# Linear attention with a dense layer, twice over: query tiles earlier in the last blocks, the last one behind the sums

## The chip, the core and the metric

The kernel runs on one core of one Trainium2 chip. The metric is the device time of one execution in microseconds (us). PE is TensorE, DVE is VectorE, ACT is ScalarE, POOL is GpSimd, SP is SyncE, which only issues DMAs here.

## The reference

Two layers follow one another twice (A, B, A, B), each with a residual. A is linear attention with the hedgehog feature map, B is dense, mish, dense. S = 2048 rows, D = 640, H = 32 heads of 20, F = 1536, everything in float32.

```python
def A(x, wqkv, w_phi, wo):
    q, k, v = split_heads(x @ wqkv)                   # 32 heads of 20
    pq, pk = q @ w_phi, k @ w_phi                     # per head, 20 x 20
    phi_q = concat(softmax(pq), softmax(-pq))         # 40 features a head
    phi_k = concat(softmax(pk), softmax(-pk))
    kv, z = phi_k.T @ v, phi_k.sum(rows)              # sums over all 2048 rows
    return merge_heads((phi_q @ kv) / (phi_q @ z + 1e-6)) @ wo

def B(x, w1, b1, w2):
    return mish(x @ w1 + b1) @ w2                     # mish: x * tanh(softplus(x))
...
# each layer's output is added to its input; a layer norm without weights stands before each
```

## The kernel before

Every product of float32 numbers is made of three matmuls of halves: a value is split into a high and a low part, and h times wh, h times wl and l times wh are summed in PSUM (`project_half`, L408 to L415). A projection of one tile of 128 rows has 2 halves of columns, 5 slices of the inner dimension and 3 products: 30 matmuls.

The 2048 rows are 8 blocks (NB) of 2 tiles (BT), tile number i from 0 to 15. Attention runs in two passes, since the averages need the sums over all keys. The first pass, `attend_first`, goes over the blocks. Each block has six pieces of work: key tiles k0 and k1, value tiles v0 and v1, query tiles q0 and q1. The tuple `order` says in which order PE projects them. The product with `w_phi` has been folded into the key and query weights at the start (`fold_part`, `fold_high`, `fold_low`, the section under `written()`).

Each piece is a generator. Its first step projects. `features` then takes five steps: ACT copies the projection out of PSUM into the tile `e`; DVE takes maximum and minimum, and POOL (queries) or DVE (keys) subtracts; ACT takes the exponential; DVE sums and inverts; POOL multiplies. `advance()` moves every pending generator by one step for each new piece. A key tile ends with 32 small matmuls into `kva` (L488), a PSUM bank that holds the sums over all keys. A query tile ends with a transpose on DVE and four stores by SP to the DRAM buffer `e_d` (L505).

What sets the order around the change:

- In `attend_first` a scheduler puts the instructions of each engine in order; `issue_after` ties one behind another. In the section under `written()` and, for PE and SP, in the second pass, the order is that of the code.
- PSUM has two double-bank tiles for projections (`mm_tile`) and four single banks (`one_tile`), one of which is `kva` during the first pass.
- Query tiles use two SBUF buffers, one for even and one for odd tiles (`query_tile`), so tile i reuses that of tile i - 2.
- In the last block `order` leaves out q1. The generator `rest()` (L687) projects this last query tile in pieces, which the second pass calls up between its own steps with `next(rest)`.

The second pass, `attend_second` (L740), begins with `finish_kv`: ACT copies `kva`, PE transposes it in three pieces (L731), DVE multiplies them by a mask into `kvb` (L734). `average(b, t)` then has 44 small matmuls (L764) with the query features that were loaded back from `e_d` (`load_groups`, L716), and DVE divides. After it come the projection with `wo`, the residual and the norm for layer B.

Of the kernel before, what the change touches and what calls it, by code (L numbers as in the profile page):

```python
# [21 lines left out]
DH = 20  # L22
# [3 lines left out]
BT = 2  # L26
# [18 lines left out]
def kernel(  # L45
# [412 lines left out]
    def attend_first(layer, x_src, first):  # L458
# [16 lines left out]
                except StopIteration:  # L475
                    pending.remove(g)

        def keys(xts, i, v):
            e = big_tile()
            yield from features(project(xts, i % BT, kv_ws, 0, w=QC), e, False)  # L480
            yield
            if i % BT == 0 and BT < i < NT - BT:
                yield
            for r in range(9):
                for j in range(4):
                    h = 3 * (4 * (r // 3) + j) + r % 3
                    if h < H:
                        nc.tensor.matmul(kva[32 * j:32 * j + DH + 1, 40 * r:40 * r + 40],  # L488
                                         v[:, (DH + 1) * h:(DH + 1) * (h + 1)], e[:, 40 * h:40 * h + 40],
                                         start=(i == 0 and r == 0), stop=(i == NT - 1), skip_group_check=True)  # L490

        def queries(xts, i, ps=None):
            e = query_tile(i)
            yield from features(project(xts, i % BT, q_ws, 0, w=QC) if ps is None else ps, e, True)

            b, t = divmod(i, BT)
            if i == NT - BT - 1:
                yield
                with tc.issue_after(last_recip[0]):
                    nc.vector.transpose(e, e)  # L500
            else:
                nc.vector.transpose(e, e)
            dst = e_d[b].rearrange("(j f) (t q s) -> t q f j s", f=32, t=BT, s=32)
            for q in range(4):
                nc.sync.dma_start(dst[t, q], e[32 * q:32 * q + 32].rearrange("f (j s) -> f j s", s=32))  # L505
                if b == NB - 1:
                    yield
# [15 lines left out]
        if first is None:  # L523
            with written():
                xt = fetch(x_src, 0)
                bd = big_tile()[:120, :720].rearrange("p (t c) -> p t c", t=6)
                nc.sync.dma_start(bd[:, :3], phi_bd[:, :3])
                raw_q = load_raw(0, range(3))

                nc.vector.memset(bd[:80, 5, :80], 0.0)  # L530
                nc.sync.dma_start(bd[:40, 5, :40], phi_bd[80:120, 4, 80:120])
                nc.sync.dma_start(bd[40:80, 5, 40:80], phi_bd[:40, 5, :40])
                nc.sync.dma_start(bd[:, 3:5], phi_bd[:, 3:5])
                shift_phi(bd, slice(0, 3))
                raw_q += load_raw(0, range(3, 6))
                kv_ws = [r1_pair(k) for k in range(KD)]
                raw_v = [fetch_v(k) for k in range(KD)]
                raw = load_raw(1)
                early = fetch(x_src, 1)
                mvs = [norm_stats(t, xt) for t in range(BT)]  # L540
                norm_scale(0, mvs)
                shift_phi(bd, slice(3, 5))
                shift_phi(bd, 5)

                q_ws = [r2_pair(k) for k in range(KD)]
                mm = [mm_tile(), mm_tile()]
                pcs = [mm[0][:, 0], mm[0][:, 1], mm[1][:, 0], mm[1][:, 1], one_tile()]
                for t in range(3):
                    for k in range(KD):
                        fold_part(pcs[k], k, t, bd, raw_q)  # L550
                xn = [row_tile() for _ in range(BT)]
                act(xn[0], xt[:, 0, :], AF.Identity, bias=stats[:, 0, 1, 0:1], scale=stats[:, 0, 0, 0:1])
                nc.vector.tensor_scalar(xn[1], xt[:, 1, :], stats[:, 0, 0, 1:2], stats[:, 0, 1, 1:2],
                                        op0=ALU.mult, op1=ALU.add)

                def highs(c, ks):
                    for k in ks:
                        fold_high(q_ws, pcs[k], k, c)

                def lows(c, ks):  # L560
                    for k in ks:
                        fold_low(q_ws, pcs[k], k, c)

                def make_v(k, low):
                    split(kv_ws[k][0][:, D:2 * D], kv_ws[k][1][:, D:2 * D], raw_v[k], low)

                def half(c, ks):
                    project_half(q0[c], nxt, 0, q_ws, 0, c, ks, w=QC)

                highs(0, (0, 1))  # L570
                lows(0, (0, 1))
                nxt = Transposed(xn)
                nxt.turn(one_tile())
                nxt.high()
                nxt.lower()
                highs(0, (4,))
                lows(0, (4,))
                pcs[0], pcs[1] = one_tile(), one_tile()
                for k in (0, 1):
                    fold_part(pcs[k], k, 3, bd, raw_q)  # L580
                mm = mm_tile()
                nxt.turn(mm[:, 0])
                nxt.turn(mm[:, 1])
                highs(0, (2,))
                nxt.high()
                highs(0, (3,))
                nxt.high()
                lows(0, (2, 3))
                nxt.lower()
                nxt.lower()  # L590
                for t in (4, 5):
                    for k in (0, 1):
                        fold_part(pcs[k], k, t, bd, raw_q)
                highs(1, (0, 1))
                q0 = [one_tile()]
                half(0, (0, 1))
                mm = mm_tile()
                pcs[2], pcs[3] = mm[:, 0], mm[:, 1]
                for k in (2, 3):
                    for t in range(3, 6):  # L600
                        fold_part(pcs[k], k, t, bd, raw_q)
                lows(1, (0, 1))
                half(0, (2, 3))
                make_v(0, nc.gpsimd)
                highs(1, (2, 3))
                lows(1, (2, 3))
                pcs[4] = one_tile()
                for t in range(3, 6):
                    fold_part(pcs[4], 4, t, bd, raw_q)
                half(0, (4,))  # L610
                make_v(1, nc.gpsimd)
                highs(1, (4,))
                lows(1, (4,))
                q0.append(one_tile())
                half(1, range(KD))
                for k in (2, 3, 4):
                    make_v(k, nc.vector)
            nc.sync.dma_start(mask, bass.AP(tensor=head_mask.tensor, offset=head_mask.offset,
                                            ap=[[1, 120], [120 * (DH + 1), 3]]))
        else:  # L620
            nxt, kv_ws, turn = first
            with tc.issue_after(last_load[0]):
                load_k_weights(kv_ws)
            q_ws = load_q_weights()
        for b in range(NB):
            xts = nxt
            order = ("k0", "k1", "v0", "v1", "q0", "q1")
            if b == 0 and layer:
                order = ("v0", "k0", "k1", "v1", "q0", "q1")
            elif b == 0:  # L630
                order = ("q0", "v0", "v1", "k0", "q1", "k1")
            elif b == 1 and not layer:
                order = ("k0", "q0", "k1", "v0", "q1", "v1")
            elif b == NB - 1:
                order = ("k0", "k1", "v0", "v1", "q0")
            vs = [v_tile() for _ in range(BT)]
            if 2 <= b < 2 + KD and not layer:
                with tc.issue_after(last_act[0]):
                    o_ws.append(next(o_gen))
                spill_o_weights(b - 2, o_ws[-1])  # L640
            for n, (kind, t) in enumerate(order):
                t = int(t)
                i = b * BT + t
                if b == 0 and layer == 0 and n in (2, 3):
                    fold_phi(kv_ws, bd, raw, ((0, 0), (1, 0), (2, 0), (3, 0)) if n == 2 else
# [8 lines left out]
                if b + 1 < NB:  # L654
# [3 lines left out]
                        nxt = xt if layer else normed(b + 1, xt)  # L658
                    elif n > 2:
                        nxt.step()  # L660
                g = {"k": lambda: keys(xts, i, vs[t]), "q": lambda: queries(xts, i, q0 if i == 0 and not layer else None),
                     "v": lambda: values(xts, i, vs[t])}[kind]()
                if b == 0 and not layer:
                    with tc.issue_after(last_product[0]):
# [21 lines left out]

        def rest():  # L687

            ps = [one_tile(), one_tile()]
            project_half(ps[0], xts, 1, q_ws, 0, 0, w=QC)  # L690
            advance()
            advance()
            yield
            project_half(ps[1], xts, 1, q_ws, 0, 1, range(2), w=QC)
            yield
            project_half(ps[1], xts, 1, q_ws, 0, 1, range(2, 4), w=QC)
            yield
            project_half(ps[1], xts, 1, q_ws, 0, 1, range(4, KD), w=QC)
            pending.append(queries(xts, NT - 1, ps))
            next(pending[-1])  # L700
            while pending:
# [38 lines left out]
    def attend_second(x_src, x_dst, acc, fetches, makes, fetch_next, begin_next):  # L740
# [61 lines left out]
        with tc.manual_schedule(engines={mybir.EngineType.PE, mybir.EngineType.SP}):  # L802
# [1 line left out]
            next(rest)  # L804
            next(kv)
            loaded[1] = begun[0] + load_groups(1, 5) + begun[1]
            next(rest)
            next(kv)
            next(rest)
            average(0, 0)  # L810
# [303 lines left out]
```

## Time and profile before

| | |
|---|---|
| runs | 1360.11, 1357.13, 1360.85 us, median 1360.11 |
| the profiled execution's own time | 1360.29 us |
| its span | 1358.5 us |
| mean granted clock of PE | 0.999 |
| instructions in the span | 30980 |
| DMA | 174.11 MB, mean 128 GB/s |

The span is what the profiler saw of the execution, from the first instruction to the last; 1.8 us lie around it. Busy times are sums over an engine's instructions, and a line number is a line of the kernel. In the view of waits a row says which engine stood still at which line, what it waited for, how long in all, how often, and the longest. The word "issue" stands where the trace shows nothing that it waited for. In the view of time a row begins with start and length, and in brackets stand the idle time before it and what ended it. SPq is the queue of SP, and its rows are the issues of DMAs. In the view of stretches the columns are the stretch, its length, busy time and number of instructions of PE, PEld (loading of weights), DVE, ACT and POOL, the granted clock, the DMA share and GB/s. The first pass of layer 0 ends near 247 us, that of layer 1 near 907 us.

### The profile page before, as it was taken

The numbers are of one execution on the slowest core, as the hardware profiler recorded it, in microseconds if no ns is written. First come the engines' busy times: TensorE is split into PE (matmuls) and PEld (weight loads), VectorE is DVE, ScalarE is ACT, GpSimd is POOL, SyncE is SP. The second block draws the span as 40 slices with busy tenths as digits, with TensorE's granted clock in tenths as the row PEclk, the third lists the DMA queues.
The fourth block names the chain that finished last, engine by engine and source line by source line (L and its number), as shares of the span: only waits on it lengthen the run. The fifth ranks groups of instructions, "written<-read, shape, count | busy, mean of one in ns | idle before, by whom it ended". The sixth has DMA issues, their size and how long they took to land.

```text
span 1358.5 us, 30980 instructions
## 1 busy us (share of the span) xinstructions
PE 1349.6 (99%) x12896; PEld 1339.3 (99%) x12896; DVE 1058.6 (78%) x1797; ACT 576.1 (42%) x968; POOL 466.2 (34%) x419
## 2 busy tenths in 40 slices
PE   9999999999999999999999999999999999999999
PEld 9999999999999999999999999989999999999998
DVE  5988988886787888778768888778668776677775
ACT  5444444322554555455443344332236444454443
POOL 3355544434322222122226556634251211111112
PEclk9999999999999999999999999999999999999999
DMA  9544444797613443334574435456974221333200
GB/s 335 162 101 91 94 113 98 183 298 271 217 28 88 117 117 88 55 93 113 147 224 97 114 79 102 86 141 215 285 254 132 78 65 41 90 98 97 68 31 20
DMA packets 352629, 174.11 MB, mean 128 GB/s; under 512 B 287449, under 2 KB 324041, under 8 KB 352489
## 3 DMA queue, kind: packets, MB, share of 16 engines
q1 hardware_dynamic: 352489, 172.14, 46.7%
q8 instruction: 101, 1.65, 0.5%
q14 instruction: 39, 0.32, 0.1%
HBM read 106.23 MB, written 65.86 MB: 127 GB/s over the span
## 4 chain that ended last, share of the span: by engine, by line
PE 93%; DVE 5%; POOL 1%; DMA 1%; issue 0%; ACT 0%; SPq 0%; POOLq 0%; DVEq 0%
PE mm L414 25%; PE one L889 25%; PE mm L940 24%; PE one L414 11%; PE mm L764 2%; PE one L334 2%; PE one L488 2%; DVE r L448 1%; PE one L940 1%; DMA raw<-in_w 1%; DVE xn L777 1%; DVE m L439 0%; PE mm L263 0%; PE one L92 0%; DVE r L442 0%
## 5 line engine op out<-in xcount | busy, mean ns | idle before, releaser
L940 PE MATMUL mm<-r2h,ol 128*128 128x320 f32 x1240 | 296.1, 309 | 0.0
L915 POOL TENSOR_TENSOR ol<-big,ol 128x512 fp32r<-128x512 f32 (+1 forms) x98 | 130.9, 1336 | 477.9 <-ACT ol L914 419.7
L889 PE MATMUL one<-xtl,r1h 128*128 128x256 f32 x960 | 268.2, 279 | 0.0
L889 PE MATMUL one<-xth,r1l 128*128 128x256 f32 x960 | 268.0, 279 | 0.0
L889 PE MATMUL one<-xth,r1h 128*128 128x256 f32 x960 | 265.9, 279 | 0.0
L940 PEld LDWEIGHTS mm<-r2h,ol 128*128 128x128 f32 x1240 | 212.5, 188 | 0.0
L940 PE MATMUL mm<-r2l,ol 128*128 128x320 f32 x620 | 191.2, 309 | 0.0
L414 PE MATMUL mm<-r1h,xth 128*128 128x304 f32 (+1 forms) x600 | 185.1, 309 | 0.0
L414 PE MATMUL mm<-r1l,xth 128*128 128x304 f32 (+1 forms) x600 | 183.8, 306 | 0.0
L414 PE MATMUL mm<-r1h,xtl 128*128 128x304 f32 (+1 forms) x600 | 183.5, 306 | 0.2 <-POOL xtl L351 0.2
L889 PEld LDWEIGHTS one<-xtl,r1h 128*128 128x128 f32 x960 | 180.4, 188 | 0.0
L889 PEld LDWEIGHTS one<-xth,r1l 128*128 128x128 f32 x960 | 180.4, 188 | 0.0
L889 PEld LDWEIGHTS one<-xth,r1h 128*128 128x128 f32 x960 | 179.6, 188 | 0.0
L904 DVE TENSOR_SCALAR big<-big 128x512 f32<-128x512 f32 (+1 forms) x98 | 57.2, 583 | 110.0 <-ACT big L902 109.8
L906 ACT ACTIVATE big<-big,two 128x512 f32<-128x512 f32 (+1 forms) x98 | 70.1, 716 | 116.1 <-DVE big L905 116.1
L914 ACT ACTIVATE ol<-big 128x512 fp32r<-128x512 f32 (+1 forms) x98 | 60.9, 622 | 137.6 <-DVE big L913 137.5
L902 ACT ACTIVATE big<-one,b1s 128x256 f32<-128x256 f32 x192 | 80.8, 467 | 89.4 <-PE one L889 88.9
L450 POOL TENSOR_TENSOR r<-r,r 128x1280 f32<-128x1280 f32 x32 | 77.2, 2411 | 116.6 <-DVE r L449 88.5
L940 PEld LDWEIGHTS mm<-r2l,ol 128*128 128x128 f32 x620 | 116.5, 188 | 0.0
L414 PEld LDWEIGHTS mm<-r1h,xth 128*128 128x128 f32 x600 | 112.8, 188 | 0.9
L414 PEld LDWEIGHTS mm<-r1h,xtl 128*128 128x128 f32 x600 | 112.8, 188 | 0.4 <-POOL xtl L351 0.4
L414 PEld LDWEIGHTS mm<-r1l,xth 128*128 128x128 f32 x600 | 112.8, 188 | 0.1
(160 smaller groups left out, 3148.9 us busy)
## 6 DMA issues: line engine op xcount, KB each, us to landing
e_d<-r SPq DMA_DIRECT2D x128, 160.0 KB, 4.1
big<-e_d SPq DMA_DIRECT2D x32, 640.0 KB, 7.2
x_d<-xt SPq DMA_DIRECT2D x23, 640.0 KB, 4.5
xt<-x_d SPq DMA_DIRECT2D x22, 640.0 KB, 4.9
n_d<-xn SPq DMA_DIRECT2D x168, 80.0 KB, 2.4
xt<-in_x SPq DMA_DIRECT2D x16, 640.0 KB, 4.3
xn<-x_d SPq DMA_DIRECT2D x28, 320.0 KB, 4.3
v<-n_d SPq DMA_DIRECT2D x30, 256.0 KB, 3.0
```

What stands on the lines that cost most here:

```text
L334: nc.tensor.transpose(ps[:, c, t * P:(t + 1) * P], self.rows[t][:, (c0 + c) * P:(c0 + c + 1) * P], ident)
L414: last_product[0] = nc.tensor.matmul(ps[:, :w], a[:, sl], r, start=(k == 0 and n == 0), stop=(k == KD - 1 and n == 2)).ins
L450: nc.gpsimd.tensor_tensor(eg, eg, r.unsqueeze(2).to_broadcast([P, 2 * H, DH]), op=ALU.mult)
L488: nc.tensor.matmul(kva[32 * j:32 * j + DH + 1, 40 * r:40 * r + 40], v[:, (DH + 1) * h:(DH + 1) * (h + 1)], e[:, 40 * h:40 * h + 40], start ...
L764: nc.tensor.matmul(po[c][64 * q:64 * q + 64, GW * j:GW * j + w], phs[g][:n, s0:s0 + 64], kvb[:n, g, :w], start=True, stop=True)
L889: nc.tensor.matmul(ph[:, j, :], l, r, start=(n == 0), stop=(n == 3 * KD - 1))
L902: exps[0] = nc.scalar.activation(part(ta, 0)[:, j - js.start], ph[:, j, :], AF.Exp, bias=b1s[:, 2 * pr + j:2 * pr + j + 1]).ins
L904: nc.vector.tensor_scalar_min(e, e, E_CAP)
L906: nc.scalar.activation(r, n, AF.Ln, bias=two)
L914: nc.scalar.activation(ah[:, js], n, AF.Copy)
L915: nc.gpsimd.tensor_tensor(al[:, js], n, ah[:, js].bitcast(F32), op=ALU.subtract)
L940: ins = nc.tensor.matmul(pys[t][c][:, :HC], (ah, ah, al)[n][:, j, t * P:(t + 1) * P], w, start=(f == 0 and n == 0), stop=(f == KF - 1 and ...
```

## The change

Three parts. First, the last four blocks get their own orders, with query tiles further ahead. Keys of the first tile of block 6 take two more idle steps before their sums, so that the value tile they need is there (`keys` now takes the list `vs` and reads it at that time). The value tiles of the last block are allocated later. The separate late transpose of tile 13 goes.

Second, `rest()` no longer projects a half tile ahead of the last key sums. The 30 matmuls now stand behind them, in pieces of 9, 9 and 12, and one call of `next(rest)` falls away.

Third, in the start section the first chunk of the query fold takes a single bank and the others the two double tiles; before, the last chunk had the single bank. The splits and transposes are put in another order to fit.

```diff
-        def keys(xts, i, v):
+        def keys(xts, i, vs):
             e = big_tile()
             yield from features(project(xts, i % BT, kv_ws, 0, w=QC), e, False)
             yield
             if i % BT == 0 and BT < i < NT - BT:
-                yield
+                for _ in range(3 if i == NT - 2 * BT else 1):
+                    yield
...
-                                         v[:, (DH + 1) * h:(DH + 1) * (h + 1)], e[:, 40 * h:40 * h + 40],
+                                         vs[i % BT][:, (DH + 1) * h:(DH + 1) * (h + 1)], e[:, 40 * h:40 * h + 40],
...
             b, t = divmod(i, BT)
-            if i == NT - BT - 1:
-                yield
-                with tc.issue_after(last_recip[0]):
-                    nc.vector.transpose(e, e)
-            else:
-                nc.vector.transpose(e, e)
+            nc.vector.transpose(e, e)
...
-                pcs = [mm[0][:, 0], mm[0][:, 1], mm[1][:, 0], mm[1][:, 1], one_tile()]
+                pcs = [one_tile(), mm[0][:, 0], mm[0][:, 1], mm[1][:, 0], mm[1][:, 1]]
...
-                highs(0, (0, 1))
-                lows(0, (0, 1))
+                highs(0, (0, 1, 2))
+                lows(0, (0,))
                 nxt = Transposed(xn)
                 nxt.turn(one_tile())
                 nxt.high()
+                lows(0, (1, 2))
                 nxt.lower()
-                highs(0, (4,))
-                lows(0, (4,))
+                highs(0, (3, 4))
                 pcs[0], pcs[1] = one_tile(), one_tile()
                 for k in (0, 1):
                     fold_part(pcs[k], k, 3, bd, raw_q)
-                mm = mm_tile()
-                nxt.turn(mm[:, 0])
-                nxt.turn(mm[:, 1])
-                highs(0, (2,))
-                nxt.high()
-                highs(0, (3,))
-                nxt.high()
-                lows(0, (2, 3))
-                nxt.lower()
-                nxt.lower()
+                nxt.turn(one_tile())
                 for t in (4, 5):
                     for k in (0, 1):
                         fold_part(pcs[k], k, t, bd, raw_q)
+                last = mm_tile()
+                nxt.turn(last[:, 0])
+                nxt.high()
+                nxt.high()
+                lows(0, (3, 4))
+                nxt.lower()
+                nxt.lower()
...
-                pcs[4] = one_tile()
+                pcs[4] = last[:, 1]
...
-            elif b == NB - 1:
-                order = ("k0", "k1", "v0", "v1", "q0")
-            vs = [v_tile() for _ in range(BT)]
+            elif b >= NB - 4:
+                order = (("k0", "k1", "v0", "q0", "q1", "v1"), ("k0", "k1", "q0", "q1", "v0", "v1"),
+                         ("k0", "q0", "q1", "k1", "v0", "v1"), ("k0", "k1", "q0", "v0", "v1"))[b - NB]
+            vs = []
...
+                if n == (3 if b == NB - 1 else 0):
+                    vs += [v_tile() for _ in range(BT)]
...
         def rest():
 
-            ps = [one_tile(), one_tile()]
-            project_half(ps[0], xts, 1, q_ws, 0, 0, w=QC)
             advance()
             advance()
+            ps = [one_tile(), one_tile()]
+            project_half(ps[0], xts, 1, q_ws, 0, 0, range(3), w=QC)
             yield
-            project_half(ps[1], xts, 1, q_ws, 0, 1, range(2), w=QC)
+            project_half(ps[0], xts, 1, q_ws, 0, 0, range(3, KD), w=QC)
+            project_half(ps[1], xts, 1, q_ws, 0, 1, range(1), w=QC)
             yield
-            project_half(ps[1], xts, 1, q_ws, 0, 1, range(2, 4), w=QC)
-            yield
-            project_half(ps[1], xts, 1, q_ws, 0, 1, range(4, KD), w=QC)
+            project_half(ps[1], xts, 1, q_ws, 0, 1, range(1, KD), w=QC)
             pending.append(queries(xts, NT - 1, ps))
...
             loaded[1] = begun[0] + load_groups(1, 5) + begun[1]
-            next(rest)
             next(kv)
```

More of the change, by code (lines that the diff above doesn't have):

```diff
@@ L660, in attend_first @@
                         nxt.step()
-                g = {"k": lambda: keys(xts, i, vs[t]), "q": lambda: queries(xts, i, q0 if i == 0 and not layer else None),
+                g = {"k": lambda: keys(xts, i, vs), "q": lambda: queries(xts, i, q0 if i == 0 and not layer else None),
                      "v": lambda: values(xts, i, vs[t])}[kind]()
```

## The prediction

> **What bounds the kernel now.** The page's engine line comes first, then the waits of PE (engine, line, what it waited for: us in all, times, longest).
>
> ```profile
> PE 1349.6 (99%) x12896; PEld 1339.3 (99%) x12896; DVE 1058.6 (78%) x1797; ACT 576.1 (42%) x968; POOL 466.2 (34%) x419
> PE mm L764 <- issue: 2.8, 2, 2.4
> PE one L92 <- POOL ident masks.py:199: 1.3, 1, 1.3
> PE mm L334 <- DVE r2l L283: 0.4, 1, 0.4
> PE one L334 <- DVE r1l L283: 0.3, 1, 0.3
> PE mm L263 <- DVE r2l L283: 0.3, 1, 0.3
> PE mm L414 <- POOL xtl L351: 0.2, 1, 0.2
> ```
>
> PE is the bound: busy 1349.6 of the 1358.5 us span, 99%. All its waits sum to 5.3 us, and the change keeps number and kind of PE's instructions. So a reordering can gain only what PE idles, and the question is which new waits it makes. I therefore go to the stretches that are edited, by the view of stretches (start:end, length, busy time of PE, PEld, DVE, ACT, POOL, then granted clock, DMA share, GB/s).
>
> ```profile
> 0.00:10.00 10.00, 8.66 (x52) 8.66 (x53) 3.09 (x12) 2.21 (x2) 2.60 (x11) 1.00 0.82 267
> 110.00:230.00 120.00, 120.00 (x1440) 118.71 (x1439) 104.64 (x133) 52.92 (x75) 62.27 (x51) 1.00 0.46 102
> 760.00:886.00 126.00, 126.00 (x1474) 124.85 (x1472) 102.04 (x112) 48.55 (x71) 76.13 (x61) 1.00 0.47 94
> 917.20:922.20 5.00, 5.00 (x60) 4.75 (x60) 4.32 (x13) 1.36 (x3) 0.00 (x0) 0.66 0.93 304
> ```
>
> Rows two and three hold blocks 4 to 6 of layer 0 and of layer 1, the blocks whose tiles are reordered. PE is busy in every microsecond of both: nothing can be gained there, and every wait made there is a loss in full. What can be gained lies at the start (0.3 + 0.4) and behind layer 1's sums: the issue wait of 2.8, and the 5.0 us after it at a granted clock of 0.66, which cost 5.0 x 0.34 = 1.7. Together 5.2 us.
>
> **Part 1, the orders of blocks 4 to 7.** A query tile's copy out of PSUM (ACT) fills one of two buffers, by parity, and it must wait until the four stores of the tile before in that buffer have landed. The view of time of ACT, layer 1 then layer 0 (start, length, instruction, idle before it and what ended it), and ACT's sum for that wait:
>
> ```profile
> ACT r L135 <- DMA e_d<-r: 74.2, 17, 6.5
> 796.32 0.68 ACT L135 ACTIVATE r<-mm 128x608 f32<-128x608 f32 x1 [3.30 <-DMA e_d<-r]
> 801.79 0.68 ACT L135 ACTIVATE r<-mm 128x608 f32<-128x608 f32 x1 [4.49 <-DMA e_d<-r]
> 813.43 0.71 ACT L135 ACTIVATE v<-mm 128x640 f32<-128x640 f32 x1 [2.40 <-PE mm L414]
> 822.25 0.68 ACT L135 ACTIVATE r<-mm 128x608 f32<-128x608 f32 x1 [2.04 <-POOL big L450]
> 828.17 0.68 ACT L135 ACTIVATE r<-mm 128x608 f32<-128x608 f32 x1 [4.93 <-DMA e_d<-r]
> 857.62 0.68 ACT L135 ACTIVATE big<-mm 128x608 f32<-128x608 f32 x1 [1.93 <-PE mm L414]
> ...
> 131.61 0.68 ACT L135 ACTIVATE r<-mm 128x608 f32<-128x608 f32 x1 [2.34 <-PE mm L414]
> 150.38 0.71 ACT L135 ACTIVATE v<-mm 128x640 f32<-128x640 f32 x1 [0.78 <-PE mm L414]
> 159.91 0.68 ACT L135 ACTIVATE r<-mm 128x608 f32<-128x608 f32 x1 [2.34 <-PE mm L414]
> 167.20 0.68 ACT L135 ACTIVATE r<-mm 128x608 f32<-128x608 f32 x1 [6.34 <-DMA e_d<-r]
> 193.31 0.68 ACT L135 ACTIVATE r<-mm 128x608 f32<-128x608 f32 x1 [4.02 <-DMA e_d<-r]
> 196.76 0.68 ACT L135 ACTIVATE big<-mm 128x608 f32<-128x608 f32 x1 [2.14 <-PE mm L414]
> ```
>
> What is to be seen is that these copies come late already: 17 of them waited for a landing, 74.2 us in all. One buffer's loop (copy, normalisation, transpose, stores, landing, next copy) is 822.25 - 796.32 = 25.9 and 828.17 - 801.79 = 26.4 in layer 1; 159.91 - 131.61 = 28.3 in layer 0, 193.31 - 167.20 = 26.1 later. PE escapes only because it has two PSUM buffers for projections and works one tile ahead. How fast does PE ask? From the chain of waits:
>
> ```profile
> 777.40 25.80 PE mm L414 x180
> 804.61 25.78 PE mm L414 x180
> 905.60 1.48 PE L488 MATMUL one<-big,v 128*21 128x40 f32 x128
> 957.11 2.70 PE mm L764 x88
> ```
>
> A block is 804.61 - 777.40 = 27.2, six projections of 25.8/6 = 4.3 and 1.4 of key sums. Before, each query buffer is asked for every 27.2 us, just above the loop of 26. In each of blocks 4, 5 and 6 the new order puts q0 one place earlier: five places from the query before, 27.2 - 4.3 = 22.9. The loop doesn't fit into that.
>
> Block 4 of layer 1 step by step (k0, k1, v0, q0, q1, v1). The stores that both copies await are of block 3, and up to there the changed program has the same order on DVE, POOL and SP, so the copies stay at 822.25 and 828.17. v0's projection ends at 813.4, q0's at 817.7, q1's at 822.0. v1 needs q0's PSUM, free at 822.25 + 0.68 = 822.9: PE waits 1.0. v1 ends at 827.3; k0 of block 5 needs q1's PSUM, free at 828.9: 1.6 more, 2.6. In layer 0 (steps of 4.7, with the transposes): v0 150.4, q1 159.8, q0's copy done 160.6, 0.8; v1 165.1, q1's copy done 167.9, 2.8; 3.6.
>
> To the end of block 6 (k0, q0, q1, k1, ...): q0's copies follow one another by 26.0, at 822.25, 848.25 and 874.25, and k1, two tiles behind, starts at 874.9 at the earliest. At the old pace k0 ends at 857.6, q0, q1 and sums take 2 x 4.3 + 1.4, k1 starts at 867.6: 7.3 us lost in layer 1. Layer 0: 159.91 + 2 x 26.0 + 0.7 = 212.6 against 196.76 + 2 x 4.7 + 1.4 = 207.6: 5.0 lost (9.4 with loops of 28.2). In block 7 q0 is again six places on, and nothing more is added. Sum 12.3. Bounds: 6.2 if the loop shrinks to the pace asked for, so that only block 4's waits remain (2.6 + 3.6); 16.7 with the long loop in layer 0. I take 12.3: three of the four loops shown are near 26.
>
> **Part 2, the last query tile behind the sums.** Each row is a time, a length and an instruction around layer 1's last sums (SPq: SP's queue; the last row: the issue-to-landing times of the loads in that stretch).
>
> ```profile
> 903.68 2.37 POOL L450 TENSOR_TENSOR big<-big,r 128x1280 f32<-128x1280 f32 x1
> 907.94 0.49 PE L731 MATMUL one<-ident,xn 128*120 128x128 f32 x3
> 908.47 1.01 DVE L734 TENSOR_TENSOR kvb<-one,mask 120x252 f32<-120x252 f32 x3 [0.33 <-PE one L731]
> 902.83 1.45 DVE L500 STREAM_TRANSPOSE r<-r 128x1280 f32<-128x1280 f32 x1
> 904.35 3.24 SPq L505 DMA_DIRECT2D e_d<-r  x4
> 907.70 4.70 SPq L716 DMA_DIRECT2D big<-e_d  x3
> DMA to landing us min/median/max: 5.4/7.2/9.5
> 917.07 0.20 PE L764 MATMUL mm<-kvb,ol 80*64 80x42 f32 x1 [2.36 <-issue]
> ```
>
> The 15 matmuls of `rest()` are only moved, 15 x 25.8/180 = 2.15 us. They stood ahead of the last sums and covered POOL's normalisation of the last key tile, which ended at 906.05, 0.45 behind the start of the sums: there was no slack. POOL may come to it sooner, since a query tile's work no longer stands in front. Between 0 and 2.15 in each layer; I take 0.4, POOL's old lag, twice: 0.8.
>
> The new wait is on SP. Before, all four stores of the last even query tile (904.35) went out ahead of the load of block 1's second half (907.70). That tile's transpose now stands behind the three products into `kvb` on DVE, and on SP its first store stands ahead of the same load, which is held with everything queued after it. From the end of the sums, T: nine matmuls (1.3), transposes and products (909.48 - 907.94 = 1.5), T + 2.8; transpose 1.45, T + 4.3; a store's issue 3.24/4 = 0.8, the load at T + 5.1; landed at the earliest 5.4 later, T + 10.5. PE: two averages (2.7) from T + 3.1, twelve matmuls (1.7), ten instructions of the next average (0.3): T + 7.8. Wait 2.7, by the median landing 4.5. I take 2.7 in each layer, the fastest, because the load is then the first of those queued: 5.4. Bounds 0 (the load goes out early enough all the same) and 9.0.
>
> The old issue wait has no releaser in the trace, so it may go or stay: from -4.5 (0.46 + 2.36 + 1.7 of clock) to 0, I take half, -2.3. A new wait as long as 2.36 may lower the clock again as that one did; I charge it once, 1.7 (bounds 0 and 1.7 for each new wait). The Trainium skill, "TensorE: Matmul & The Clock Gate", section "What's actually happening", has the clock halved after an idle window of about 3.4 us; the trace doesn't agree, since here 2.36 us sufficed, and the measurement decides. By that page this term would be 0 and the sum 1.7 lower.
>
> **Part 3, the start.** The same fold instructions, the first chunk in its own bank, so its split can begin before a neighbour's sums. PE's two waits for splits, 0.4 and 0.3, are what it can save: I take -0.7, bounds -1.0 (the last 0.3 too) and 0. The 1.3 for the identity stays.
>
> **Sum.** -0.7 + 12.3 + 0.8 + 5.4 - 2.3 + 1.7 = 17.2 on the profiled execution's 1360.3 (its span 1358.5 plus 1.8 outside; 0.2 above the median of the runs): 1377.5.
>
> **Rivals.** (1) Faster: the query waits are absorbed. For it: ACT waited up to 6.3 us for a landing there and PE never idled. Against it: the hand walk, in which the one spare PSUM buffer is just what is used up. Decides if the loop falls below 22.9 from block 4 on. Then start and issue wait count alone: 1360.3 - 0.7 - 4.5 = 1355.1. (2) About the same: block 4's waits stay (6.2), later loops shrink because the tile's normalisation is also asked for earlier, and the load lands under cover: 1360.3 + 6.2 - 5.2 = 1361.3. For it: a loop holds time in which DVE and POOL do other tiles. Against: the stores and landing in it don't shrink. (3) Far slower: each new wait in parts 1 and 2, some eight of 1 to 3 us, is followed by 5 us of a lowered clock as after the 2.36; seven more of 1.7, 11.9: 1389.4. Against it: the stretch 0 to 10 holds a wait of 1.3 and its clock is 1.00. The issue wait could also be the filling of instructions: the Trainium skill, "Runtime: NRT & Kernel Launch", section "Instruction fetch mechanics", says that an engine's instructions are fetched in blocks by DMA, mostly hidden. No row here shows such a fetch's end; if it is one, its place moves with the instruction count and not with the waits, which is why I keep half.
>
> **Chances.** The forecast 0.58, rival 1 0.14, rival 2 0.14, rival 3 0.14. A measurement of this kernel tells some 0.3% from no change, 4.1 us: faster below 1356.0, slower above 1364.2. Rival 1 gives faster 0.14; rival 2 mostly the same, 0.10; the rest, 0.76, slower. The range leaves out rival 1 and the top of rival 3: 1358 to 1390.
>
> **What the changed profile would show.** PE waits of 1 to 3 us on L414 projections in blocks 4 to 6 of both layers, released by ACT's copy that waited for a landing of `e_d`; 120 us of full PE becoming 115 or less. An average of block 1 waiting for its load, whose issue is held behind the first store of tile 14. The start shortened by 0.7. I'm wrong if query copies in blocks 5 and 6 follow one another by 23 us instead of 26, or if PE shows no wait there.

## The result, and the profile after

The changed kernel takes 1393.34 us (median of 5 runs, 1392.0 to 1394.77) against 1360.11: a ratio of 1.0251, 95% interval 1.0236 to 1.0266. It is slower, as forecast, but by 33 us instead of 17, and above the range that was given (1358 to 1390). The profiled execution took 1392.0 us, its span is 1390.2, 31.7 more than before.

First the engine line of the changed kernel's page and the waits of PE (engine, line, what it waited for: us in all, times, longest). L489 is the line of the key sums here, L760 that of the averages.

```profile
PE 1358.0 (98%) x12896; PEld 1345.3 (97%) x12896; DVE 1065.4 (77%) x1797; ACT 575.2 (41%) x968; POOL 467.9 (34%) x419
PE mm L414 <- ACT r L135: 17.1, 9, 3.7
PE mm L760 <- DMA big<-e_d: 5.7, 2, 3.3
PE one L489 <- POOL big L450: 3.3, 3, 1.5
PE one L92 <- POOL ident masks.py:199: 1.3, 1, 1.3
PE one L334 <- DVE r1l L283: 0.9, 1, 0.9
PE one L263 <- issue: 0.3, 1, 0.3
PE mm L414 <- POOL xtl L351: 0.2, 1, 0.2
```

The three rows on top are new, and each is a wait that the prediction named: projections wait for ACT's copy of a query tile, averages wait for their load, the last sums wait for POOL. The waits sum to 28.8 instead of 5.3 us, 23.5 more. PE's busy time has grown by 8.4 with the same number of instructions. 23.5 + 8.4 = 31.9 is, within rounding, the whole difference of the spans (31.7).

The view of time of PE shows where the nine waits for copies lie, layer 0 first (start, length, instruction, idle time before it and what ended it).

```profile
160.40 0.42 PE L414 MATMUL mm<-r1h,xth 128*128 128x320 f32 x1 [0.87 <-ACT r L135]
167.44 0.41 PE L414 MATMUL mm<-r1h,xth 128*128 128x304 f32 x1 [2.37 <-ACT r L135]
194.31 0.63 PE L414 MATMUL mm<-r1h,xth 128*128 128x320 f32 x1 [2.71 <-ACT r L135]
222.50 0.42 PE L414 MATMUL mm<-r1h,xth 128*128 128x320 f32 x1 [2.35 <-ACT r L135]
...
839.88 0.41 PE L414 MATMUL mm<-r1h,xth 128*128 128x320 f32 x1 [1.00 <-ACT r L135]
845.87 0.41 PE L414 MATMUL mm<-r1h,xth 128*128 128x304 f32 x1 [1.32 <-ACT r L135]
865.68 0.41 PE L414 MATMUL mm<-r1h,xth 128*128 128x320 f32 x1 [0.79 <-ACT r L135]
872.42 0.41 PE L414 MATMUL mm<-r1h,xth 128*128 128x320 f32 x1 [2.08 <-ACT r L135]
896.48 0.40 PE L414 MATMUL mm<-r1h,xth 128*128 128x304 f32 x1 [3.65 <-ACT r L135]
```

Block 4 came as walked through by hand: 0.87 + 2.37 in layer 0 where 3.6 was forecast, 1.00 + 1.32 in layer 1 where 2.6 was. Blocks 5 and 6 together lost 5.1 in layer 0 and 6.5 in layer 1, where 1.4 and 4.7 were forecast. Why they lost more is seen in ACT's copies of the query tiles, the odd ones (tiles 9, 11, 13) of layer 0 and the even ones (8, 10, 12) of layer 1, and in DVE's transposes of tiles 8 and 10 in layer 1:

```profile
166.70 0.68 ACT L135 ACTIVATE r<-mm 128x608 f32<-128x608 f32 x1 [4.71 <-DMA e_d<-r]
193.58 0.68 ACT L135 ACTIVATE r<-mm 128x608 f32<-128x608 f32 x1 [5.25 <-DMA e_d<-r]
221.77 0.68 ACT L135 ACTIVATE r<-mm 128x608 f32<-128x608 f32 x1 [5.62 <-DMA e_d<-r]
...
839.15 0.68 ACT L135 ACTIVATE r<-mm 128x608 f32<-128x608 f32 x1 [6.25 <-DMA e_d<-r]
864.95 0.68 ACT L135 ACTIVATE r<-mm 128x608 f32<-128x608 f32 x1 [7.74 <-PE mm L414]
895.75 0.68 ACT L135 ACTIVATE r<-mm 128x608 f32<-128x608 f32 x1 [12.21 <-DMA e_d<-r]
...
857.08 1.50 DVE L498 STREAM_TRANSPOSE r<-r 128x1280 f32<-128x1280 f32 x1
885.50 1.45 DVE L498 STREAM_TRANSPOSE r<-r 128x1280 f32<-128x1280 f32 x1
```

Behind block 4 the prediction followed q0, the even buffer, alone. In blocks 5 and 6 of layer 0 it is the odd buffer's loops that PE waits for: 193.58 - 166.70 = 26.9 and 221.77 - 193.58 = 28.2, against the 26.0 taken. In layer 1 the even buffer's loop was 864.95 - 839.15 = 25.8 (that copy waited for PE's projection, not for the buffer, so the buffer itself took no longer) and then 895.75 - 864.95 = 30.8. In the first round the transpose began 17.9 us behind the copy (857.08), in the second 20.6 (885.50), so 2.6 of the 5.0 more were lost before the transpose, the rest between the transpose and the landing. A tile's steps are called one by one with the following pieces of work, and these were held up by the waits themselves. That this is why the step came later is read from the code and not tried apart.

The clock is the other part. These are rows of the view of stretches (start:end, length, busy time of PE, PEld, DVE, ACT, POOL, granted clock, DMA share, GB/s), behind the waits that end at 167.44, 194.31, 872.42, 896.48 and 948.38:

```profile
168.00:169.00 1.00, 1.00 (x9) 1.00 (x9) 1.00 (x3) 1.00 (x2) 0.03 (x1) 1.00 0.00 0
195.00:196.00 1.00, 1.00 (x5) 1.00 (x5) 1.00 (x3) 1.00 (x4) 1.00 (x1) 0.50 0.00 0
873.40:876.70 3.30, 3.30 (x15) 3.30 (x14) 3.16 (x4) 2.99 (x7) 2.57 (x3) 0.50 0.07 15
897.30:900.60 3.30, 3.30 (x15) 3.30 (x14) 1.60 (x3) 0.00 (x0) 1.27 (x1) 0.50 0.63 99
948.50:951.70 3.20, 3.20 (x33) 3.12 (x34) 1.60 (x6) 0.60 (x1) 0.00 (x0) 0.50 1.12 353
```

In five places (a wait of 2.40 ahead of an average in layer 0 is the fifth) the clock stood at 0.50 for 3.4 us, which costs 1.7 each, 8.5 together. A wait of 2.08 was followed by a fall, one of 2.37 was not; e7_clock below shows why.

Last the end of the first pass in layer 1, with SP's queue:

```profile
935.96 0.83 PE L489 MATMUL one<-big,v 128*21 128x40 f32 x64 [0.94 <-POOL big L450]
942.42 0.32 SPq L501 DMA_DIRECT2D e_d<-r  x1
942.85 2.01 SPq L712 DMA_DIRECT2D big<-e_d  x3
948.38 1.32 PE L760 MATMUL mm<-kvb,big 120*64 120x63 f32 x20 [3.25 <-DMA big<-e_d]
```

The load of block 1's second half went out at 942.85, right behind the first store of tile 14, and the average waited 3.25 for it (2.40 in layer 0). The old issue wait of 2.8 is gone.

### The profile page after: what moved, and what is told of

Same layout as the page of the kernel before. It is cut to its first block, busy times and chain, and to the rows that moved or that the text cites. A ratio compares the mean times of both kernels' runs of the same rounds, so it can differ in the third digit from the quotient of the medians.

```text
span 1390.2 us, 30978 instructions
## 1 busy us (share of the span) xinstructions
PE 1358.0 (98%) x12896; PEld 1345.3 (97%) x12896; DVE 1065.4 (77%) x1797; ACT 575.2 (41%) x968; POOL 467.9 (34%) x419
## 4 chain that ended last, share of the span: by engine, by line
PE 75%; DVE 11%; DMA 5%; POOL 3%; SPq 3%; issue 2%; ACT 1%; DVEq 0%; ACTq 0%; POOLq 0%
PE one L884 24%; PE mm L935 24%; PE one L414 11%; PE mm L414 10%; DMA e_d<-r 3%; SPq L501 3%; DVE r L448 2%; PE mm L760 2%; DVE m L439 2%; PE one L334 2%; DVE r L498 2%; DVE big L440 1%; POOL r L450 1%; DVE big L442 1%; DMA xt<-in_x 1%
## 5 line engine op out<-in xcount | busy, mean ns | idle before, releaser
L414 PE MATMUL mm<-r1h,xth 128*128 128x304 f32 (+1 forms) x600 | 188.1, 314 | 17.1 <-ACT r L135 17.1
L414 PE MATMUL one<-r2h,xth 128*128 128x320 f32 (+1 forms) x350 | 111.2, 318 | 0.0
```

The lines of the kernel that those rows point to most:

```text
L414: last_product[0] = nc.tensor.matmul(ps[:, :w], a[:, sl], r, start=(k == 0 and n == 0), stop=(k == KD - 1 and n == 2)).ins
```

## The experiments

The theory: the loss has three places, the loop of the two query buffers in blocks 4 to 6, the load behind a store, and the last sums without their cover; and a wait of a few microseconds costs more than itself because it can halve the clock. The rival: the end of the first pass or the rate of the engines is what counts. Each part of the change was first put alone into the kernel before.

**e1_orders, blocks 4 to 6 alone.**

```diff
+            elif b >= NB - 4:
+                order = (("k0", "k1", "v0", "q0", "q1", "v1"), ("k0", "k1", "q0", "q1", "v0", "v1"),
+                         ("k0", "q0", "q1", "k1", "v0", "v1"), ("k0", "k1", "v0", "v1", "q0"))[b - NB]
...
+                for _ in range(3 if i == NT - 2 * BT else 1):
+                    yield
```

> Only the orders of blocks 4 to 6 (and the two idle steps of tile 12's keys) are changed. Theory L (a query tile's copy waits for the landing of the tile two before it in the same buffer, and PE waits for the PSUM that the copy frees): the nine PE waits for ACT's copies that the changed kernel shows, 17.1 us in all, return, and three of those longer than 1.7 us are followed by 3.4 us of half clock, 1.7 us each: 1360 + 17 + 5 = 1382, range 1377 to 1388; the issue wait behind layer 1's sums stays. Theory E (the loss comes from the end of the first pass, the orders alone cost little): 1360 to 1366.

Measured: 1380.84 us, ratio 1.0158 (1.0137 to 1.0178). The waits are back, nearly in number and size (17.1 in 9 in the changed kernel):

```profile
PE mm L414 <- ACT r L135: 18.1, 10, 3.9
PE mm L766 <- issue: 0.3, 1, 0.3
```

The orders alone cost 21 us; theory E is out. The second row was not expected: the issue wait behind layer 1's sums has shrunk to 0.3, in the same average.

**e2_last, the last block's order and `rest()` alone.**

```diff
-                order = ("k0", "k1", "v0", "v1", "q0")
+                order = ("k0", "k1", "q0", "v0", "v1")
...
+            project_half(ps[0], xts, 1, q_ws, 0, 0, range(3), w=QC)   # rest() as in the change
```

> Only the last block's order and the last query tile behind the sums are changed, blocks 4 to 6 stay as before. Theory L: two waits of an average for its load (2.4 + 3.3), PE waiting for POOL ahead of the last sums (3.3), two falls of the clock (3.4), less the issue wait and its clock (4.5): 1360 + 7.9 = 1368, range 1364 to 1371. Theory E: 1376 or more, since this is where the loss comes from.

Measured: 1381.74 us, ratio 1.0161 (1.0143 to 1.0179), 22 us slower where 8 were expected. PE's waits in it:

```profile
PE mm L414 <- ACT r L135: 9.7, 2, 5.2
PE one L488 <- POOL big L450: 5.5, 4, 1.5
PE mm L760 <- DMA big<-e_d: 3.5, 2, 3.2
```

My number for the orders' theory missed a case of its own mechanism. With block 6 unchanged, q0 of block 7 comes four places behind q0 of block 6 instead of six, 27.2 - 2 x 4.3 = 18.6 us, against a loop of 26: one wait of 4.46 and one of 5.20. In the whole change block 6 has its queries early, and these two waits are absent. The two parts are therefore not additive (21 + 22 against 33 together): the early queries of blocks 4 to 6 pay for the early one of block 7. The clock did more here as well. It fell three times, as often as it fell for e1_orders, but each time for 6.8 us instead of 3.4. This is the first of the three in the view of stretches; the wait of 4.46 had begun at 238.9 and ended at 243.37, inside it:

```profile
241.51:248.33 6.82, 4.96 (x18) 4.96 (x19) 4.91 (x5) 3.87 (x6) 1.45 (x3) 0.50 0.67 103
```

**e3_start, the start alone.** The edit is the diff's third part.

> Only the start section is changed. By the prediction's step 0.7 us are gained: 1359.4. By the trace of the changed kernel, in which the same copies of layer 0 come 0.2 to 0.35 us earlier: 1359.8. The rival, that the freed bank costs a wait elsewhere in the start: 1361 or more.

Measured: 1357.8 us, ratio 0.999 (0.9979 to 1.0001). If it gains, it gains about 1.5 us, twice the step's 0.7, but no change lies within the interval. In the trace the start's three waits of 0.4, 0.3 and 0.3 are gone, and others of 0.9, 0.3 and 0.2 stand in their place, so PE's waits there are not shorter.

**e4_bigq, more buffers.** The disputed mechanism taken away: the changed kernel with the queries of blocks 4 to 6 in the five buffers that key tiles rotate through.

```diff
-            e = query_tile(i)
+            e = big_tile() if NB - 4 <= i // BT < NB - 1 else query_tile(i)
```

> The changed kernel, but the query tiles of blocks 4 to 6 take the five rotating buffers of the key tiles instead of the two query buffers, so that a buffer comes round after five tiles, some 34 us, instead of two. Theory L: the PE waits for copies in blocks 4 to 6 go (17.1) with three falls of the clock (5.1): 1393 - 22 = 1371, range 1367 to 1376. Rival R (not the buffer but the rate of ACT, DVE and POOL, or of the stores, limits these blocks): 1388 or more, with the same waits.

Measured: 1371.77 us, ratio 1.009 (1.0075 to 1.0106). Of the 17.1 us of waits for copies none is left, and the new order of tiles is the same:

```profile
PE mm L760 <- DMA big<-e_d: 5.7, 2, 3.8
PE one L489 <- POOL big L450: 4.2, 4, 1.5
PE mm L414 <- POOL xtl L351: 2.6, 3, 1.5
```

So it is the buffers, and neither the rate of ACT, DVE and POOL nor the stores as such. PE's busy time fell with them, from 1358.0 to 1351.4. The other two terms are still there (5.7 and 4.2, against 5.7 and 3.3), and projections that wait for POOL have grown from 0.2 to 2.6, a price of this edit.

**e5_load and e6_cover, the end of the first pass.** On top of e4_bigq, first the transpose and stores of tile 14 one step later, then also the 15 matmuls ahead of the sums again.

```diff
             b, t = divmod(i, BT)
+            if i == NT - BT:
+                yield
             nc.vector.transpose(e, e)
```

> As e4_bigq, and the transpose and stores of the last even query tile (14) come one step later, so that on SP the load of block 1's second half goes out ahead of them. If the load is held by the store in front of it, as the prediction had it, the two waits of an average for its load in e4_bigq (3.8 + 1.9) go, with one or two falls of the clock (1.7 each): 1371.8 - 5.7 - 2.6 = 1363.5, range 1361 to 1366. Rival (the load is late because its buffer comes free late, behind the last sums): same waits, 1370 to 1373.

Measured: 1362.37 us, ratio 1.0028 (1.0016 to 1.0041). No wait for a load is left, no fall of the clock either (mean clock 1.0). On SP the first store of tile 14 now goes out at 929.58 in layer 1, and the loads stand ahead of it from 901.78 on. 9.4 us came back from a wait of 5.7; of the rest, 3.2 are PE's busy time (1351.4 to 1348.2), since e4_bigq still had a mean clock of 0.996.

> As e5_load, and the last query tile's first half is projected ahead of the last sums again, in the pieces of the kernel before. If those 15 matmuls were the cover of POOL's last normalisation, PE's waits for POOL ahead of the sums (0.9 in layer 0, 1.1 + 1.5 in layer 1 of e4_bigq) go: 3.4 less than e5_load, 1360, range 1358 to 1362. Rival (POOL is late by its own order, not for lack of cover): same as e5_load.

Measured: 1359.5 us, ratio 1.0004 (0.9995 to 1.0013). PE waits for POOL at the sums no longer. With all three causes taken away one by one, 1393 became 1372, 1362 and 1360: the loss is accounted for, and what is left of the change (the orders with more buffers, the start) is even with the kernel before.

**e7_clock, the clock by itself.** A kernel of its own that leaves out both layers, with stretches of PE work parted by idle gaps of known length.

```python
for rep in range(16):
    for n in (128, 384, 640, ..., 2944):
        nc.tensor.transpose(ps[:, P:2 * P], dst[:, :P], ident)        # needs ACT's last copy
        for _ in range(60 + 3 * (rep % 5)):
            nc.tensor.transpose(ps[:, :P], ident, ident)
        nc.scalar.activation(few, ps[:, :8], AF.Copy)
        nc.scalar.activation(dst[:, :n], src[:, :n], AF.Copy)         # the gap
```

> None of the layers is computed: x is copied to the output while PE runs stretches of 11 to 14 us of transposes, 192 in all, parted by idle gaps of twelve lengths, some 0.8 to 3.8 us, in which it waits for an ACT copy. Theory G (windows of 3.41 us on a fixed grid; the clock is halved for one window when PE was idle for over half of the one before): no fall below 1.7 us of idle, a fall behind a share w/3.41 of the gaps of length w between 1.7 and 3.4 (a half at 1.7, 0.7 at 2.4, 0.9 at 3.1), all of them above 3.4; each lasts 3.4 us at 0.50. Rival S (a whole window of idle is needed): no falls below 3.4. Rival D (a fixed length decides): none below some 2.0, all above 2.4.

Its one run took 1817.51 us. The gaps came out between 0.5 and 2.9 us. Five of them in the view of time, and the stretches at the lowered clock that began at 72.5, 82.7, 92.9 and 113.4:

```profile
71.14 0.33 PE L39 MATMUL ps<-ident,dst 128*128 128x128 f32 x1 [2.02 <-ACT dst L43]
81.92 0.33 PE L39 MATMUL ps<-ident,dst 128*128 128x128 f32 x1 [2.23 <-ACT dst L43]
92.91 0.48 PE L39 MATMUL ps<-ident,dst 128*128 128x128 f32 x1 [2.44 <-ACT dst L43]
104.10 0.33 PE L39 MATMUL ps<-ident,dst 128*128 128x128 f32 x1 [2.66 <-ACT dst L43]
113.85 0.47 PE L39 MATMUL ps<-ident,dst 128*128 128x128 f32 x1 [2.87 <-ACT dst L43]
...
72.50:75.90 3.40, 3.40 (x18) 3.40 (x17) 0.00 (x0) 0.00 (x0) 0.00 (x0) 0.50 0.00 0
82.74:86.14 3.40, 3.40 (x18) 3.40 (x17) 0.00 (x0) 0.00 (x0) 0.00 (x0) 0.50 0.00 0
92.98:96.38 3.40, 3.40 (x17) 3.40 (x18) 0.00 (x0) 0.00 (x0) 0.00 (x0) 0.50 0.00 0
113.46:116.86 3.40, 3.01 (x14) 3.01 (x15) 0.00 (x0) 0.34 (x1) 0.00 (x0) 0.50 0.00 0
```

The four falls come at 72.46, 82.70, 92.94, 113.42: 3, 3 and 6 times 3.413 us apart. All 27 falls of the run lie on that grid within 0.01 us. The gap of 2.66 that ends at 104.10 is cut by a point of the grid (103.18) into 1.74 and 0.92, and the clock stays. Counted over all windows of the grid, every window with 2.02 us of idle or more is followed by a fall and none with 1.95 or less; the three between, 1.99 without a fall and 2.00 and 2.01 with one, are too close to tell. By length of gap:

```
length of gap, us      0.5 to 1.8   2.0   2.2   2.4-2.5   2.7   2.9
gaps                       112       16    16     15       16    17
followed by a fall           0        6     8      3        4     6
```

Theory G is right in the grid and in its length, and wrong in the share: not half of a window but some 2.0 of 3.41 us. Rivals S and D fall, since gaps of 2.0 were followed by falls and 11 of 17 gaps of 2.9 were not.

The same holds in the changed kernel. Its five falls begin at 194.09, 269.19, 873.34, 897.24 and 948.44, whole steps of 3.413 us apart. Points of this grid cut the wait of 2.37 (at 166.79) into 1.72 and 0.65 and that of 2.35 (at 221.40) into 1.25 and 1.10, and no fall follows. The other five waits above 2.0, that of 2.08 too, have over 2.0 us in one window, and all five are followed by a fall.

**e8_late, e9_shift, e10_shift6 and e11_tiny, the old issue wait.** All on e3_start, which still has that wait (2.6). In e8_late two loads are put behind block 1's averages in SP's order; in the other three, more instructions stand on PE ahead of everything.

```diff
-            loaded[2] = load(2)
-            fetches[0]()
             average(1, 0)
             cur = Transposed(rows.pop(0)).all()
             average(1, 1)
+            loaded[2] = load(2)
+            fetches[0]()
...
-    for _ in range(30):                 # e9_shift: 12, and 118 transposes of 8 columns;
+    for _ in range(24):                 # e10_shift6: 24, and 32;
         nc.tensor.transpose(warm[:, :P], ident, ident)
+    for _ in range(32):                 # e11_tiny: 22, and 17 matmuls of 8 columns, two passes each
+        nc.tensor.transpose(warm[:8, :P], ident[:, :8], ident)
```

> The kernel before with the changed start section, and in the second pass block 2's loads and the first weight load are issued behind the two averages of block 1 instead of ahead of them. If the issue wait behind layer 1's sums (2.4 to 2.6, and 1.7 of clock) comes from PE's instruction fetch that stands among those loads on the DMA engines, it shrinks to the 0.3 of e1_orders: 1357.8 - 4 = 1354, range 1352.5 to 1356.5. Rival (a wait of PE's own at that instruction): 1357.8 as e3_start, or later loads make something wait: 1359 or more.

Measured: 1359.74 us, ratio 1.0003 (0.9994 to 1.0012). The issue wait is still 2.0. The edit didn't do what it was meant to: SP doesn't wait for PE, so loads that stand later in the order of the code go out nearly as early, and the DMA share during the wait was above 1.0 as before. It decides nothing about the loads.

> e3_start with 100 more instructions pairs on PE ahead of everything: the 30 warm-up transposes become 12 of 128 columns and 118 of 8 columns, about the same time. Theory F (the issue wait is PE's instruction fetch, bound to a place in its stream, slow where the loads fill the DMA engines): the wait moves 200 instructions up, to the first averages, where the DMA share was 0.6 instead of 1.1, and shrinks to some 0.5; no fall of the clock: 1357.8 - 2 - 1 = 1354.5, range 1353 to 1357. Rival P (the wait belongs to that place in the program): it stays where it was, 1357 to 1359.

Measured: 1366.87 us, ratio 1.0062 (1.0046 to 1.0077), slower where a gain was expected. In the trace the issue wait behind layer 1's sums is 0.3, but the start pays for it. A transpose of 8 columns into 128 took 14.36/118 = 0.12 us, as long as a whole one (ten of layer 1 took 1.31 us in the kernel before):

```profile
3.96 14.36 PE L94 MATMUL one<-ident 128*8 128x128 f32 x118
926.10 0.86 PE L764 MATMUL mm<-kvb,big 120*64 120x63 f32 x23 [0.30 <-issue]
```

> As e9_shift with 26 more pairs (24 transposes of 128 columns, 32 of 8). Theory F: the wait moves 52 instructions up, into the first half of the average before, or ahead of it, where the loads already fill the engines, and keeps its 2 to 2.6 us: 1357 to 1359. Rival P: it stays at the last group of the average, the fourth instruction from its end.

Measured: 1358.72 us, ratio 1.0 (0.999 to 1.001). The wait is gone altogether, not moved up; the average now waits 1.2 for its load. The start was later too, the first fold at 10.11.

> e10_shift6 without its cost at the start: the same 26 more pairs of instructions on PE ahead of everything, but as 22 warm-up transposes and 17 matmuls of 8 columns in two passes each, in about the time of the 30 before. Theory F (the wait is bound to a place in PE's stream of instructions): no issue wait of over 1 us behind layer 1's sums, the first fold as early as in e3_start; a wait of an average for its load of some 1.2 stays: 1358.7 - 2 = 1356.7, ratio 0.998 to the kernel before, 1355 to 1358. Rival P: the issue wait is back, 1358.

Measured: 1362.3 us, ratio 1.0021 (1.0012 to 1.003). Again no issue wait in the averages, and again a later start: the first fold began at 10.09 instead of 6.76 in e3_start, and the clock fell there, behind a window in which PE had no idle time:

```profile
6.66:10.07 3.41, 3.41 (x32) 3.41 (x32) 1.05 (x4) 0.92 (x1) 1.83 (x7) 1.00 1.05 349
10.07:13.48 3.41, 3.41 (x18) 3.41 (x18) 0.00 (x0) 0.00 (x0) 0.13 (x3) 0.50 1.04 325
```

So three shifts of PE's stream took the wait away, and e8_late, with the stream unshifted, kept it. That speaks for the place in the stream, but it isn't shown: each shift also made the start later by 3 to 11 us, and e1_orders, with the stream of the same length up to there but the averages at another time, had 0.3 at the same place. That the fetch of instructions behind the loads is what makes it long stays open as well, since e10_shift6 lost the wait entirely where theory F expected it to move. In the traces of the three runs with the long wait a 16 KB DMA packet of the kind `instruction` stands at its start: 914.4 in the kernel before, where the wait began at 914.7, 913.6 in e3_start (913.8) and 915.8 in e8_late (916.3). In e10_shift6 such a packet came earlier, at 910.3, and no issue wait followed. That agrees with a fetch, but whose instructions the packet holds the profile doesn't say.

## Why the prediction was right in direction and wrong in size

It forecast the side, the three new waits and their places. Its range missed by 3.3 us. Two steps failed most: the clock, which was charged for one new wait only ("I charge it once, 1.7"), and the constant loop of 26.0 in the query waits. The first fell short by 6.8 us, the second by 4.8. Point by point, for the profiled execution:

- **Query waits: 12.3 forecast, 17.1 measured.** Mechanism and block 4 were right (2.6 + 3.6 = 6.2 forecast, 5.6 measured), and e4_bigq shows the cause. The step that failed is the constant loop of 26.0, "three of the four loops shown are near 26": the loops had been read where PE ran without waits, and under the new order they took up to 28.2 in layer 0 (8.3 lost there, 5.0 forecast) and 30.8 into block 6 of layer 1 (8.8 lost, 7.3 forecast). The odd buffer, which the walk to the end of block 6 left out, ended three of the five later waits. The bound of 16.7 was also below what came. q0 of block 7 stands seven places behind q0 of block 6 in the new order, not six; no wait hangs on that.
- **Load behind the store: 5.4 forecast, 5.7 measured**, with e5_load as the evidence that SP's order is the cause.
- **Cover of the last sums: 0.8 forecast, 3.3 measured** (2.4 in layer 0, just above its bound of 2.15, and 0.9 in layer 1). I took POOL's old lag; e6_cover shows that the 15 matmuls were what covered it.
- **The issue wait: -2.3 forecast, -4.5 measured** (2.8 and its fall of the clock). Half had been taken, and it went; why it went stays open.
- **The clock: +1.7 forecast, five falls measured, 8.5.** This is the largest miss, and rival 3, which had 0.14, is nearest to the truth (1389.4). It is near in part by luck: it counted eight falls where five came, and longer waits made up for the other three. It had been dismissed by a wait of 1.3 without a fall, which says nothing on waits of 2 to 3.7. By e7_clock a wait below 2.0 costs itself, and a longer one costs 1.7 more if some 2.0 of it fall into one window. By the grid above that sorts the seven waits over 2.0 into the five with a fall and the two without. The Trainium skill, "TensorE: Matmul & The Clock Gate", section "What's actually happening", speaks of a free-running window of 3413 ns; the grid of e7_clock agrees with it. That the slow state needs a whole idle window does not agree: 2.0 of the 3.41 us were enough.
- **The start: -0.7 forecast, some -0.3 in the profiled execution** (layer 0's copy of tile 6 at 131.26 instead of 131.61), though PE's waits there grew by 0.2, and e3_start can't tell it from nothing.

The terms as measured: 17.1 + 5.7 + 3.3 of new waits, 0.2 more at the start (2.7 against 2.5), less the issue wait of 2.8, are the 23.5; five falls less the old one are 6.8 of the 8.4 by which PE was busy longer. The remaining 1.6 I can't place.

## What to carry to other kernels

Before moving work ahead, measure the loop of the buffer that it fills, from one filling to the next and with the landing of its stores, and set it against the new distance: here 26 us, and up to 31 once waits held up its steps, against 22.9, and no wait showed beforehand because a spare PSUM buffer hid it. Look for the wait of the engine that is *not* the bound (74.2 us on ACT here): it tells how little is left. And price a wait of TensorE with its clock. By the runs here a wait among full matmuls costs nothing extra while it is below 2 us; above that it cost a fall of 1.7 us or more when some 2 us of it fell into one window of the grid.

## What the runs showed of the hardware that was not expected

- TensorE's clock is decided on a grid of 3.413 us that goes on through the whole run. In e7_clock 27 of 27 falls lay on it, each lasted one step at 0.50, and some 2.0 us of idle within one step decided. A fall can last longer: in e2_last three lasted two steps, 6.8 us.
- It isn't idle time alone that is counted. In the profile of the kernel before, the fall began at 918.74 (the row below, of its view of stretches), so its window began at 915.33, and the issue wait ended at 917.07: 1.74 us of idle, among the short matmuls of the averages, sufficed there. In e11_tiny the clock fell at 10.07 behind a window without any idle time, which held matmuls of 8 columns. What is counted was not tried further.

```profile
918.74:922.15 3.41, 3.41 (x47) 3.33 (x44) 2.91 (x9) 0.52 (x2) 0.00 (x0) 0.50 0.90 269
```

- PE can stand still for 2 to 2.6 us with nothing that the profile shows. The wait was gone when PE's stream had been moved by 52 instructions (e10_shift6), and 0.3 with other orders of the blocks ahead of it (e1_orders). The cause stays open.
- A transpose of an 8-column slice against a 128-column identity took 14.36/118 = 0.12 us (e9_shift), and a pass of a matmul that sends only 8 columns through a 128-column identity took as long: 34 of them 4.15 us (e11_tiny).
